# Loading the weights of a two-layer kernel through one queue, in the order keys, queries, values, output

## The chip, the cores and the metric

The kernel runs on one core of a Trainium2 chip. A core has five engines that follow their own instruction queues: TensorE (PE in the profile) multiplies matrices, VectorE (DVE) and ScalarE (ACT) work elementwise, GpSimd (POOL) builds masks and issues transfers, and SyncE (SP) does nothing here but issue transfers. Transfers between the chip's memory and the core's own memory run on 16 DMA engines, which serve the queues of SyncE, ScalarE and GpSimd. An instruction that must wait, for a transfer or for another engine, holds back everything behind it in its engine's queue.

The metric is the device time of one execution in microseconds. Before the change it is 1650.74 us, the median of three runs (1646.95 to 1651.44).

## The reference

Tokens `x` (2048 rows of 512 numbers) pass through four blocks: A, B, A, B, each with a layer normalisation in front and a residual sum behind it. Block A is attention with a small memory that is carried from segment to segment. With 32 heads of 128 and the mask "memory rows see all, tokens see what is not later":

```
mem = mem0                                   # 8 rows
for s in range(64):                          # segments of 32 tokens
    h = concat(mem, x[32 tokens of segment s])        # 40 rows of 512
    q, k, v = h @ Wq, h @ Wk, h @ Wv                  # 512 -> 32 x 128 each
    p = softmax(mask(q @ k.T * 128**-0.5))
    o = (p @ v) @ Wo                                  # 32 x 128 -> 512
    mem = o[:8]
    out[segment s] = o[8:]
```

The next segment's first eight rows are this segment's result, so the 64 segments follow each other strictly. Block B is linear attention over all 2048 tokens: `qkv = x @ wqkv`; with phi(t) = t + 1 above zero and exp(t) below it (and 1e-6 more), `kv = sum phi(k) v`, `z = sum phi(k)`, `o = phi(q) kv / (phi(q) z)`, and `o @ wo`. The same weights serve both rounds. Inputs and outputs are bf16.

## The kernel before

All weights are loaded once, at the start, and stay in the core: `Wq_sb`, `Wk_sb`, `Wv_sb` (4 MB each, partition = row of a 128-row chunk, in runs of 8 KB), `Wo_sb` (4 MB, in four loads of 8 heads, runs of 1 KB) and B's input weights `wqkv_sb` (1.5 MB). B's output weights `MB_sb` are loaded by GpSimd (`load_wo_b`, L970).

The work of block A is organised by segment (64 steps) and by tile of 128 tokens (4 segments). `prepare` (L1179) normalises a tile, transposes it with TensorE (L1075) and writes it as `hT`; `left_block` (L1138) projects the last 8 tokens of all four segments at once; `project` (L1098) is the projection of one segment: for each of four chunks of 128 rows, matmuls of the segment's rows against 512 columns of a weight, L1117 for the first and L1038 (`again`) for the following ones, which use the same loaded rows. Queries and keys are always projected together in one such instruction group, which waits for both weights. Values are projected by a group of their own. `mem_attention` (L1190) and `x_attention` (L1265) form the scores, their exponentials (ScalarE) and the weighted sums (L1050 on TensorE, L1238 and L1260 on VectorE); `out_proj` (L1339, matmuls L1353) multiplies by `Wo_sb` and waits for all four loads of it; `next_mem` (L1369) hands the eight rows on; `residual` (L1400) sends the results to their tokens with small transfers that GpSimd issues (L945). `evac` (L933) copies from the matmul accumulators, on ScalarE (L929) or VectorE (L930).

The order of the work is not found while the program runs. Every instruction is a node with a key (layer, step, name, number), and `when` (L572) looks up a time for it in two tables: `OWN` (L187) for particular steps and `PERIOD` (L19) for steps that repeat. `schedule` (L690) sorts all nodes by these times; each engine's queue is that order cut down to its own nodes. The times only sort: an instruction runs when it is at the head of its queue and what it waits for is done. The costs and latencies given to `add` (L642) are notes of a planner and do not act at run time. `finalize` (L727) turns the dependencies (`reads`, `writes`, `after`) into semaphore waits.

The start is the group with the key (0, -9, "setup"). Its first entries are the loads, in the order of the code from L955 to L971: SyncE issues the memory rows `A_mem0` and the first 128 tokens; ScalarE issues queries, keys and values, which the table sorts as values (-43583), queries (-12468), keys (-10416); SyncE issues the four output loads, the first two only after the keys have landed, the other two after the values, and then B's input weights after the output load with number 3 has landed. The table sorts the four as 1, 0, 3, 2. ScalarE's table of exponentials is loaded at L974, and all later work of ScalarE stands behind it. GpSimd loads the next two token tiles, builds constants and masks, and then stands at `load_wo_b` until B's input weights have landed.

Of the kernel before, what the change touches and what calls it, by code (L numbers as in the profile page):

```python
# [187 lines left out]
    (0, -9, 'setup'): '-23881 -2811 -12468 -10416 -43583 21376 13817 27505 24711 33310 -11418 -25383 -11486 -11353 -10564 -9986 -9510 -9028 -7908 -7700 -7486 -7329 -7314 -7002 -4822 -4403 -4292 -3436 -3097 -2480 -2001 -1544 -1040 -425 303 598 825 2114 2451 2767 3806 4244 8941 4464 5201 5238 5547 5902 10670a -9456 -7547a 39031 12088 13578 16040 16417 17105 1822 -26965',  # L188
# [6 lines left out]
    (0, 0, 'kq0'): '13808 15010 15310 17315 18082v 19746 19340a 23091',  # L195
    (0, 0, 'kq1'): '17637 18020 18543 18861 21288v 22253 21384v 23532',
    (0, 0, 'mem0'): '27658 28172 28190 29861 30676 31704 31783 32208 31967 32476',
# [12 lines left out]
    (0, 1, 'out'): '44451 44669 44741 45014 45337 45555 45773 46175 46501a 46538a',  # L210
    (0, 1, 'ql'): '32700v 32981v',
    (0, 1, 'res'): '52219 53313 54918',
    (0, 1, 'v'): '39333 40965 41700 42114 42672a 43188v',
    (0, 1, 'x'): '43625 44185 44721 45081 45683 45380 46379v 47185a 48758a 47851v 46850 47270 52096 52534 52673 53568 54508a 56814v 51794 53025 53214 53360 55042v 57491v',
    (0, 2, 'kq0'): '47407 48125 48417 49149 49383v 51153 49746a 50354',
# [5 lines left out]
    (0, 2, 'mem0'): '51902 52471 53043 53225 53347 53484 54024 54037 53671 54519',  # L221
    (0, 2, 'mem1'): '52595 52927 53142 53807 53987 54494 54953 55144 54626 55332',
    (0, 2, 'next'): '57504 57571 58118v',
    (0, 2, 'out'): '55213 55536 55596 55853 56017 56282 56453 56766 56904a 57411a',
    (0, 2, 'prep'): '7141 11551 11747 12128 13230 13879 16317v 24205a 22992v 17580a 14579a',
    (0, 2, 'ql'): '47981a 52537a',
    (0, 2, 'res'): '58281 67019 61329',
    (0, 2, 'v'): '51172 51814 51886 52975 53621v 53680a',
    (0, 2, 'x'): '54497 54743 55346 56242 56492 57902 62274a 58331v 61866a 61385a 60603 63624 63220 64197 64252 64308 64852a 69378v 63451 64157 64212 64690 65204v 66660a',
    (0, 3, 'kq0'): '58554 59210 59409 59907 60905a 60950 60138v 61209',  # L230
    (0, 3, 'kq1'): '60534 60535 60782 61428 62206a 63172 62183v 62810',
# [3 lines left out]
    (0, 3, 'out'): '65288 65592 65810 65982 66237 66316 66723 66771 67272a 67561a',  # L235
# [6 lines left out]
    (0, 4, 'mem0'): '72686 73456 74533 75009 75383 75885 77205 77353 77122 77568',  # L242
# [4 lines left out]
    (0, 4, 'res'): '80671 80824 82777 71884 72667 72775 73095 73429 74084 74354 74698 74812a 75389a 75765 80611 76852 77291 76394 79454 80754 79192 78160 84469',  # L247
    (0, 4, 'v'): '72797 75050 75264 75761 76781a 77027v',
    (0, 4, 'x'): '77272 77900 78143 78209 78737 79058 81425v 79309a 81777a 81269v 81287 81403 86062 86150 87203 87586 88466a 95437a 85646 86400 86662 86953 89440v 87687a',
# [4 lines left out]
    (0, 5, 'mem1'): '86657 86699 86929 88059 88344 88705 89233 89727 89241 90130',  # L254
# [5 lines left out]
    (0, 5, 'x'): '88077 90731 91507 91539 92846 93972 96883v 98142a 97124a 93099a 98473 95909 99150 99206 99235 99738 100206a 105270a 99879 100117 100204 100979 101797a 102570a',  # L260
    (0, 6, 'bi'): '84711 85579 85614 86087 86511 86963 86235 87472v 87874 88040 88303 88445 88757 90870 91274 114152 114458 122909 123007 125922a 126258 120139 127135 126348 123352 127014 127470 127704 127723 128959 129215 129414',
# [7 lines left out]
    (0, 6, 'mem1'): '99043 99071 99363 99702 99664 100680 101135 101181 100567 101883',  # L269
    (0, 6, 'next'): '103464 103978 104291v',  # L270
    (0, 6, 'out'): '101039 101247 101494 102002 102048 102266 102652 102763 102977a 103536a',
    (0, 6, 'prep'): '14049 14142 36561 47147 88442 88632 88768v 103149v 100817a 93747a 93965v',
    (0, 6, 'ql'): '92381a 89685a',
    (0, 6, 'res'): '104408 114484 105497',
    (0, 6, 'v'): '96416 97117 97566 98107 98450a 99368v',
    (0, 6, 'x'): '100337 101744 101969 102646 103217 103965 105837a 108154v 105947v 105369v 109602 108071 110104 110877 110951 110962 111313a 112628v 111099 111185 111472 111534 111878v 117102a',
# [4 lines left out]
    (0, 7, 'next'): '114319 114412 114889v',  # L281
# [5 lines left out]
    (0, 8, 'kq0'): '114994 115277 115928 116529 117824a 117870 118437a 118856',  # L287
# [6 lines left out]
    (0, 8, 'res'): '126874 127829 127416 118367 118620 119005 120395 120746 121165 121292 121510 121980a 122356a 122883 124485 122896 125179 122927 127002 124750 125614 127093 131320',  # L294
    (0, 8, 'v'): '119803 120314 121933 122108 122671a 123112v',
    (0, 8, 'x'): '122179 123493 123804 124525 125187 125394 125314v 128539v 127537v 125881v 133774 128307 131471 133813 134096 134138 135512v - 131116 131245 132962 134079 - 134800a',
    (0, 8, 'xl'): '89684',
    (0, 9, 'kq0'): '127940 128381 128815 129253 129992a 130193 130027v 130829',
    (0, 9, 'kq1'): '129280 129672 129761 130189 130920a 132891 130670a 132353',
    (0, 9, 'mem0'): '131377 132020 133268 133552 133420 133758 134518 134534 134256 134866',  # L300
    (0, 9, 'mem1'): '133194 133195 133862 134507 134802 135314 135480 135976 135487',
# [3 lines left out]
    (0, 10, 'bi'): '131528 132048 132423 132568 132939 133554 - 134394v 134746 134890 135163 135405',  # L305
# [12 lines left out]
    (0, 58, 'x'): '- - 760505 760834 761378 761717 765481a 762418a 766652v 761991a 767761 766509 768891 768947 769002 769058 770177a 771278a 768513 768568 768724 769776 770338v 771116a',  # L318
# [9 lines left out]
    (0, 59, 'x'): '769848 770190 770848 771439 771897 774037 772547v 772800v 772825a 773053v 775444 777039 773485 776237 776724 776779 777292a 777130a 773342 773596 777321 777377 778556a 778997a',  # L328
# [3 lines left out]
    (0, 60, 'mem1'): '779419 780681 781091 781660 781799 782529 782881 783191 782857 783541',  # L332
# [5 lines left out]
    (0, 60, 'x'): '781455 782216 782359 783392 783621 784444 784305v 784702v 784652a 784155a 786571 788051 785842 786253 786308 792585 793150a 794809a 791776 791832 791987 792266 793760v 795547v',  # L338
    (0, 61, 'kq0'): '786705 786834 787265 787696 788367v 789359 788367a 788997',
    (0, 61, 'kq1'): '788127 788558 788989 789420 790091a 790809 790572a 791249',  # L340
    (0, 61, 'mem0'): '790713 790741 791151 791539 791750 792224 792513 792949 792593 793299',
    (0, 61, 'mem1'): '791748 791887 792424 792888 793027 793303 793655 793965 793415 794315',
# [6 lines left out]
    (0, 62, 'bi'): '790202 791171 791366 791700 792549 793025 790203 794166a 795580 795796 796012 796588 797045 802425 806330 796443 817005 817236 817567 818024a 818674 818304 820023 827953 806386 806611 807178 817784 819139 820630 820951 823771',  # L349
# [7 lines left out]
    (0, 62, 'res'): '807985 809971 808991',  # L357
    (0, 62, 'v'): '800400 800831 801473 802015 803099a 802686v',
    (0, 62, 'x'): '803293 803635 804034 804871 805329 806782 806037v 805785a 805784v 806093a 807732 806926 806892 807016 807403 810316 810667a 811210v 806836 807459 811505 811563 811914v 812504a',
    (0, 63, 'kq0'): '807602 808344 809276 809587 810378v 811101 810299a 812640',  # L360
    (0, 63, 'kq1'): '808592 809885 810427 810858 812011a 812749 811529a 813111',
# [7 lines left out]
    (0, 63, 'x'): '814789 815144 815707 815910 816222 816920 817058v 817037a 817653a 817345a 817197 817942 818130 818186 818241 818297 818648a 818899 818955 819010 819066 819417v',  # L369
# [3 lines left out]
    (0, 66, 'bm'): '830386 829502 830247 830993 831337 832054 832689v 831346 831993v 831130 831586a 831838 833319a',  # L373
    (1, -6, 'bo'): '675873 795483 831613 832078 832798 833468 834212 834663 834769 834985 835444',
    (1, -4, 'start'): '660687a',
    (1, -2, 'left0'): '838552 839675 840537 841830 842501a 843585 842501v 843223',
    (1, -2, 'left1'): '838813 840106 841846 843554 844757a 845387 844275a 844906',
    (1, -2, 'lefts'): '849843 850453 850867 851285',
    (1, -2, 'leftv'): '843985 844416 844593 845278 845949a 846579 847057 846430a 847743 848013',
    (1, -2, 'prep'): '836415 836762 836957 837291 837372 838012 838482a 839279a 843047a 862887a 854362v',  # L380
    (1, 0, 'bo'): '793183 835179 838242 838490 839427 840097 849285 849741 850061 850557 852052',
    (1, 0, 'kq0'): '840968 841399 842261 843245 843794a 845749 843947v 846111',
    (1, 0, 'kq1'): '845606 846140 846295 847002 848077a 849058 847700a 848375',
    (1, 0, 'mem0'): '848295 848323 848733 849147 849285 849629 850221 850531 850277 850881',
    (1, 0, 'mem1'): '849501 849529 850006 850509 850370 850785 851137 851446 850795 851797',
    (1, 0, 'next'): '853722 853887 854257v',
    (1, 0, 'out'): '851274 851492 851710 851928 852283 852501 852856 853074 853395a 853556a',
    (1, 0, 'ql'): '845268v 846912a',
    (1, 0, 'v'): '847629 847864 848423 848737 849664a 849525v',
    (1, 0, 'x'): '850664 852162 852539 852955 853413 853752 854277a 854690v 853980a 858781a 855057 854551 859999 860055 860110 860500 861263a 863739v 859554 860199 860221 860389 861668v 863038a',  # L390
    (1, 1, 'kq0'): '854499 854930 855213 855792 856463a 857548 856463v 857186',
    (1, 1, 'kq1'): '856042 856782 857213 857645 858315v 859180 858160a 858729',
# [418 lines left out]
def _build_kernel(nc, A_x, A_mem0, A_Wq, A_Wk, A_Wv, A_Wo, A_seg_len, B_wqkv, B_wo, out):  # L811
# [112 lines left out]
    add = P.add  # L924
# [754 lines left out]
```

## Time and profile before

| | |
|---|---|
| median of three runs | 1650.74 us |
| the profiled execution's own time | 1659.31 us |
| its span, first to last instruction | 1657.6 us |
| TensorE busy | 1551.8 us, 94% of the span |
| VectorE, ScalarE, GpSimd busy | 77%, 64%, 20% |
| chain that ended last | TensorE 79%, ScalarE 8%, VectorE 7%, DMA 3% |
| mean granted TensorE clock | 0.992 |

A profile row of the timeline gives the start and the duration in microseconds, the engine (ACTq, SPq and POOLq are the issuing side of a queue, PEld is the loading of the stationary operand), the line of the kernel, the operation, the tile written and the tiles read, and in brackets the idle time of the engine before it with what ended that idle time. "pb" is the matmul accumulator; "arena" is one large tensor that holds most working tiles. Weight tiles appear by their own names, so the projections and the loads can be told apart by name. The page's first part shows where engines are busy, but the question of a start is what the first wait of each engine ended on; this is in the timeline, in the waits, and in the chain that ended last.

### The profile page before, as it was taken

To read this page: it belongs to the slowest core of one execution; us is meant where nothing else is said; L and a number is where in the kernel's file an instruction comes from. 1 tells how busy PE (TensorE), PEld (TensorE's weight loads), DVE (VectorE), ACT (ScalarE), POOL (GpSimd) and SP (SyncE) were. 2 spreads that over 40 slices of the span, in tenths; PEclk is the share of its full clock that TensorE was granted. 3 is DMA by queue.
4 is the path that set the end of the run, shared out by engine and by line. 5 is a ranking of instruction groups with operands and counts; after the bars stand their busy time and mean duration, and the time that the engine had idled before them with its cause. 6 is when DMAs were issued, how large, how long until landed. Compare 5 with 4: busy or idle time off the path is not lost.

```text
span 1657.6 us, 105934 instructions
## 1 busy us (share of the span) xinstructions
PE 1551.8 (94%) x53257; PEld 884.8 (53%) x44057; DVE 1276.4 (77%) x4017; ACT 1067.1 (64%) x3060; POOL 325.4 (20%) x660
## 2 busy tenths in 40 slices
PE   1899999999999999999799999999999999999996
PEld 0455555555555555555445555655556556555553
DVE  1677878787888787777667888787887888888766
ACT  0566666666666666666466677666767666676664
POOL 2012121222222112222102211222221221222030
PEclk9999999999999999999999999999999999999998
DMA  9300000000000000000000000000000000001013
GB/s 354 116 13 17 14 10 15 17 17 17 17 13 17 10 16 16 17 16 20 22 7 14 16 16 20 20 14 17 20 17 18 20 20 11 20 20 30 9 51 121
DMA packets 34893, 51.07 MB, mean 31 GB/s; under 512 B 13432, under 2 KB 28592, under 8 KB 32912
## 3 DMA queue, kind: packets, MB, share of 16 engines
q0 software_dynamic: 21744, 19.78, 4.1%
q1 hardware_dynamic: 11120, 11.94, 2.2%
q10 hardware_dynamic: 1584, 12.58, 1.9%
q8 instruction: 381, 6.24, 1.6%
q14 instruction: 64, 0.52, 0.1%
HBM read 29.63 MB, written 10.49 MB: 24 GB/s over the span
## 4 chain that ended last, share of the span: by engine, by line
PE 79%; ACT 8%; DVE 7%; DMA 3%; issue 2%; POOL 1%; ACTq 0%; DVEq 0%
PE pb L1117 22%; PE pb L1038 22%; PE pb L1353 16%; PE pb L1050 13%; ACT arena_sb L929 5%; DMA Wk_sb<-in_A_Wk_dram 2%; DVE arena_sb L930 2%; PE pb L1377 2%; PE pb L1211 1%; DMA dx_sb<-y_sb 1%; DVE arena_sb L1134 1%; POOL dx_sb L945 1%; PE pb L1075 1%; PE pb L1291 1%; ACT outW_sb L929 1%
## 5 line engine op out<-in xcount | busy, mean ns | idle before, releaser
L929 ACT ACTIVATE arena_sb<-pb 128x512 bf16<-128x512 f32 (+6 forms) x1068 | 505.2, 500 | 284.7 <-PE pb L1038 213.7
L945 POOL DMA_DIRECT2D dx_sb<-y_sb x504 | 252.9, 508 | 932.3 <-DVE y_sb L1388 650.3
L1050 PE MATMUL pb<-arena_sb 128*32 128x128 bf16 (+2 forms) x14320 | 404.0, 224 | 23.3 <-ACT arena_sb L929 7.3
L1117 PE MATMUL pb<-Wk_sb,arena_sb 128*32 128x512 bf16 x4096 | 413.5, 380 | 5.6 <-ACT arena_sb L929 2.9
L1038 PE MATMUL pb<-Wq_sb,arena_sb 128*32 128x512 bf16 x4096 | 413.3, 379 | 0.0
L930 DVE CAST arena_sb<-pb 128x512 bf16<-128x512 f32 (+3 forms) x647 | 335.0, 522 | 95.7 <-PE pb L1038 49.9
L1050 PEld LDWEIGHTS pb<-arena_sb 128*32 128x32 bf16 x14320 | 273.2, 96 | 200.6 <-issue 73.8
L1353 PE MATMUL pb<-Wo_sb,arena_sb 128*32 128x256 bf16 x10368 | 345.1, 273 | 6.7 <-issue 4.5
L1353 PEld LDWEIGHTS pb<-Wo_sb,arena_sb 128*32 128x32 bf16 x10368 | 264.2, 96 | 61.2 <-issue 17.8
L1134 DVE STREAM_TRANSPOSE arena_sb<-arena_sb 128x256 f32<-128x256 f32 x640 | 262.5, 431 | 25.0 <-ACT arena_sb L929 15.8
L1117 PE MATMUL pb<-Wv_sb,arena_sb 128*32 128x512 bf16 x2560 | 257.7, 378 | 0.1
L1038 PE MATMUL pb<-Wv_sb,arena_sb 128*32 128x512 bf16 x2560 | 257.6, 379 | 0.0
L1117 PEld LDWEIGHTS pb<-Wk_sb,arena_sb 128*32 128x32 bf16 x4096 | 124.7, 97 | 213.8 <-issue 169.3
L929 ACT ACTIVATE arena_sb<-arena_sb 32x256 bf16<-32x256 bf16 (+1 forms) x409 | 153.2, 378 | 22.8 <-DVE arena_sb L1298 17.2
L1117 PE MATMUL pb<-Wq_sb,arena_sb 128*32 128x512 bf16 x1024 | 107.4, 387 | 23.0 <-DMA Wk_sb<-in_A_Wk_dram 22.4
L1117 PEld LDWEIGHTS pb<-Wv_sb,arena_sb 128*32 128x32 bf16 x2560 | 76.6, 96 | 74.1 <-issue 55.7
L1228 ACT ACTIVATE arena_sb<-pb 128x192 bf16<-128x192 f32 (+1 forms) x256 | 83.8, 328 | 44.4 <-PE pb L1211 25.7
L929 ACT ACTIVATE outW_sb<-pb 128x128 fp32r<-128x128 f32 x274 | 61.9, 274 | 78.1 <-PE pb L1353 75.5
L1238 DVE TENSOR_TENSOR arena_sb<-arena_sb 128x128 bf16<-128x128 bf16 x504 | 92.7, 213 | 23.5 <-ACT arena_sb L1228 19.6
L1038 PE MATMUL pb<-Wk_sb,arena_sb 128*32 128x512 bf16 x1024 | 106.9, 386 | 0.0
L1388 DVE TENSOR_TENSOR y_sb<-pb,outW_sb 64x256 bf16<-64x256 f32 x158 | 65.8, 416 | 44.2 <-ACT outW_sb L929 39.8
L1260 DVE TENSOR_TENSOR arena_sb<-pb,arena_sb 128x128 bf16<-128x128 f32 x252 | 73.3, 291 | 34.0 <-ACT arena_sb L1249 14.7
(102 smaller groups left out, 1721.7 us busy)
## 6 DMA issues: line engine op xcount, KB each, us to landing
Wv_sb<-in_A_Wv_dram ACTq DMA_DIRECT2D x1, 4096.0 KB, 14.0
Wq_sb<-in_A_Wq_dram ACTq DMA_DIRECT2D x1, 4096.0 KB, 23.3
Wk_sb<-in_A_Wk_dram ACTq DMA_DIRECT2D x1, 4096.0 KB, 32.6
Wo_sb<-in_A_Wo_dram SPq DMA_DIRECT2D x4, 1024.0 KB, 10.4
xs_scratch<-x_sb POOLq DMA_DIRECT2D x32, 128.0 KB, 2.0
pq_scratch<-arena_sb POOLq DMA_DIRECT2D x32, 128.0 KB, 2.0
dx_sb<-y_sb POOLq DMA_DIRECT2D x252, 12.0 KB, 1.9
dx_sb<-y_sb POOLq DMA_DIRECT2D x252, 4.0 KB, 1.9
```

Source lines behind the costliest of these rows:

```text
L929: return e.activation(o() if callable(o) else o, i() if callable(i) else i, ACTF.Copy)
L930: return e.tensor_copy(o() if callable(o) else o, i() if callable(i) else i)
L945: add(eng, lambda e: e.dma_start(o, i), 0.55 if eng == "pool" else 0.4, reads=reads, writes=writes, dsem="%s%d" % (kind, k), lat=lat + (0. ...
L1038: return pe.add_instruction(mybir.InstMatmult(name=nc.get_next_instruction_name(), engine=mybir.EngineType.PE, ins=[pe.lower_ap(x), pe.low ...
L1050: r = pe.matmul(o[q], w[:, q], x, start=start, stop=stop, skip_group_check=True, tile_position=(0, 32 * j))
L1117: r = pe.matmul(o, blk[:, c, :], w, start=(c == 0), stop=(c == 3), tile_position=(0, 32 * j))
L1134: add("dve", lambda v: v.transpose(dst, src(img[:, k, :].bitcast(F32))), 0.445, reads=[("img", k)], writes=[dkey])
L1228: add("act", lambda a: a.activation(PQ[:, r2, b, 0:nq], tl.f32()[:, 0:nq], ACTF.Exp, scale=SCALE), c_act(nq), tiles=[tl], writes=[("PQ", r ...
L1238: add("dve", lambda v, a=a, p_=p_, w_=w_: v.tensor_tensor(wide(Pm[:, k, a, :]), p_.unsqueeze(2).to_broadcast([128, 4, 4, 8]), w_, ALU.mult ...
L1260: add("dve", lambda v: v.tensor_tensor(oTb[:, s % NO, 16 * b:16 * b + 16, 0:8], pv.f32()[:, 0:128].rearrange("p (n q) -> p n q", q=8), Rm[ ...
L1353: r = pe.matmul(tl.f32()[32 * j:32 * j + 32, 0:256], oT[:, 4 * hh + n, :], Wo_sb[:, 8 * n + hh, 256 * d:256 * d + 256], start=(hh == 0 and ...
L1388: add("dve", lambda v: v.tensor_tensor(y_sb[0:64, k, :], tl.f32()[0:64, 0:256], outW[64:128, w, :].bitcast(F32), ALU.add), c_dve(256), rea ...
```

## The change

SyncE's queue takes all weight loads, in the order keys, queries, values, output weights 0 to 3, B's input weights. None waits for the landing of another; only their order in the queue is fixed. The memory rows and the first tokens move to ScalarE's queue, ahead of its table load. In the `OWN` table the ten load entries become the ten smallest times. The other changed entries of the table, 154 of them, move by 1.

```
     (0, -9, 'setup'): '-23881 -2811 -12468 -10416 -43583 21376 13817 27505 24711 33310 -11418 ...      # before
     (0, -9, 'setup'): '-1000000 -999999 -999998 -999997 -999996 -999995 -999994 -999993 -999992 -999991 -11418 ...   # after
```

```diff
     P.at(0, -9, "setup")
-    add("sp", lambda s: s.dma_start(mem0_sb[0:M, :], A_mem0[0]), 0.1, writes=[MEM0], dsem="dmem", lat=2.0)
-    add("sp", lambda s: s.dma_start(x_sb[:, 0, :], x_view[0]), 0.4, writes=[("x", 0)], dsem="dx0", lat=8.5)
+    add("act", lambda a: a.dma_start(mem0_sb[0:M, :], A_mem0[0]), 0.45, writes=[MEM0], dsem="dmem", lat=2.5)
+    add("act", lambda a: a.dma_start(x_sb[:, 0, :], x_view[0]), 0.45, writes=[("x", 0)], dsem="dx0", lat=6.0)
     late = []
-    for i, (W, v, nm, t) in enumerate(((Wq_sb, qk_view[0], "Wq", 13.2), (Wk_sb, qk_view[1], "Wk", 23.7),
-                                       (Wv_sb, qk_view[2], "Wv", 34.8))):
-        late.append(add("act", lambda a, W=W, v=v: a.dma_start(W[:, :, :], v), 0.5, writes=[nm], dsem="d" + nm, lat=t))
+
+    def load(o, i, nm, lands):
+        late.append(add("sp", lambda e: e.dma_start(o, i), 0.45, writes=[nm], dsem="d%d" % len(late),
+                        lat=lands - 1.25 - 0.45 * len(late)))
+        late[-1].order.update(late[-2:-1])
+
+    for W, v, nm, t in ((Wk_sb, qk_view[1], "Wk", 14.2), (Wq_sb, qk_view[0], "Wq", 24.0), (Wv_sb, qk_view[2], "Wv", 33.8)):
+        load(W[:, :, :], v, nm, t)
     wo_view = A_Wo.rearrange("h e d -> e h d")
     for i in range(4):
         hs = slice(8 * i, 8 * i + 8)
-        add("sp", lambda s, hs=hs: s.dma_start(Wo_sb[:, hs, :], wo_view[:, hs, :]), 0.9, writes=[("Wo", i)],
-                 dsem="dWo%d" % i, after=[late[1 + i // 2]], lat=(12.5, 14.5, 7.3, 9.8)[i])
-    add("sp", lambda s: s.dma_start(wqkv_sb[:, :, :], B_wqkv.rearrange("(c p) f -> p c f", p=128)), 0.5,
-        writes=["wqkv"], dsem="dwqkv", after=[P.nodes[-1]], lat=5.0)
-    late.append(P.nodes[-1])
+        load(Wo_sb[:, hs, :], wo_view[:, hs, :], ("Wo", i), 36.9 + 3.1 * i)
+    load(wqkv_sb[:, :, :], B_wqkv.rearrange("(c p) f -> p c f", p=128), "wqkv", 50.0)
...
     P.before["act"] = add("act", lambda a: a.preload_act_table_set("natural_log_exp_and_others"), 1.3)
+    P.before["act"].order.update(P.nodes[0:2])
```

`late[-1]`, on which GpSimd's `load_wo_b` waits, is B's input weights as before.

## The prediction

> **What bounds the kernel now.** I read the DMA issues first (KB each, us from issue to landing), because the change touches nothing but loads at the start.
>
> ```profile
> Wv_sb<-in_A_Wv_dram ACTq DMA_DIRECT2D x1, 4096.0 KB, 14.0
> Wq_sb<-in_A_Wq_dram ACTq DMA_DIRECT2D x1, 4096.0 KB, 23.3
> Wk_sb<-in_A_Wk_dram ACTq DMA_DIRECT2D x1, 4096.0 KB, 32.6
> ```
>
> With the issues at 0.81, 1.28 and 1.87 us (timeline), the big weights land at 14.8, 24.6 and 34.5: values, queries, keys. The steps of 9.8 and 9.9 us show that they are served one after the other, 4.19 MB at about 425 GB/s. Next the chain that ended last, in order of time (start, duration):
>
> ```profile
> 1.87 32.59 DMA Wk_sb<-in_A_Wk_dram
> 34.50 0.62 PE pb L1117 x3
> ```
>
> and who waited for whom in the first 120 us (total us, times, longest):
>
> ```profile
> PE pb L1117 <- DMA Wk_sb<-in_A_Wk_dram: 22.4, 1, 22.4
> ...
> SPq L964 <- DMA Wk_sb<-in_A_Wk_dram: 32.9, 1, 32.9
> SPq L966 <- DMA Wo_sb<-in_A_Wo_dram: 7.3, 1, 7.3
> ...
> POOL arena_sb L971 <- DMA arena_sb<-in_B_wqkv_dram: 40.3, 1, 40.3
> ```
>
> TensorE idles 22.4 us until the keys land, and this wait is on the chain: its first 34.5 us are loading. After that TensorE is the bound (94% busy, 79% of the chain). The timeline of the start (start, duration, instruction, idle before it and its releaser):
>
> ```profile
> 9.28 0.69 DVE L1061 BATCH_NORM_STATS2 st_sb<-x_sb 128x6 f32<-128x512 bf16 x1 [7.82 <-DMA x_sb<-in_A_x_dram]
> ...
> 12.83 0.39 ACT L929 ACTIVATE arena_sb<-pb 128x96 bf16<-128x96 bf16 x2 [0.16 <-DVE arena_sb L930]
> ...
> 34.50 0.62 PE L1117 MATMUL pb<-Wq_sb,arena_sb 128*32 128x512 bf16 x4 [22.41 <-DMA Wk_sb<-in_A_Wk_dram]
> ...
> 44.80 0.10 PEld L1117 LDWEIGHTS pb<-Wv_sb,arena_sb 128*32 128x32 bf16 x4 [0.33 <-issue]
> ...
> 55.63 1.93 PE L1353 MATMUL pb<-Wo_sb,arena_sb 128*32 128x256 bf16 x64
> 55.74 0.77 POOL L971 DMA_DIRECT2D arena_sb<-in_B_wo_dram  x1 [40.30 <-DMA arena_sb<-in_B_wqkv_dram]
> ...
> 58.31 0.35 PE L1050 MATMUL pb<-arena_sb 128*32 128x128 bf16 x12 [0.76 <-ACT arena_sb L929]
> ...
> 75.45 1.03 POOL L945 DMA_DIRECT2D dx_sb<-y_sb  x2 [18.94 <-DVE y_sb L1388]
> ```
>
> It shows when each weight is wanted: queries and keys together at 34.5, values 10.3 us later, output weights 21.1 us later. The values land first and lie unused for 30 us. The tokens are ready at 13.2.
>
> **The change part by part.** The three big loads keep their size and stay in one queue; the order becomes keys, queries, values. The first matmul then needs the second load instead of the third and can start at 24.6 instead of 34.5: **gain 9.9 us**. Behind it the order of every engine is that of before: the other entries of the table move by at most 1, and where this makes or breaks a tie, the two entries belong to different engines. So I shift every row after 34.5 by 9.9 and ask which load then comes too late.
>
> Values: wanted at 44.8 - 9.9 = 34.9; as third load they land at about 34.5. **Cost 0**, with 0.4 us to spare; each us of delay beyond that costs one.
>
> Output weights: wanted at 55.6 - 9.9 = 45.7. They follow the values in the same queue, without the gap after 34.5 in which little moved. Their rate is in the stretches (last number GB/s, before it the DMA share):
>
> ```profile
> 33.00:34.00 1.00, 0.00 (x0) 0.00 (x0) 0.00 (x0) 0.00 (x0) 0.00 (x0) 1.00 0.66 270
> ...
> 41.00:42.00 1.00, 1.00 (x26) 0.22 (x12) 0.00 (x0) 0.00 (x0) 0.00 (x0) 1.00 1.02 335
> ...
> 46.00:47.00 1.00, 1.00 (x28) 0.24 (x12) 1.00 (x5) 0.25 (x1) 0.00 (x0) 1.00 1.10 347
> ```
>
> The third big load's bytes end near 33.7 (270 of 425 GB/s in that stretch). From 37 to 48 the output weights run at 345 GB/s on average, so their 4.19 MB take 12.2 us and end at 45.9. From last bytes to landing took 0.8 us for the keys and 1.5 for the last of the four output loads (bytes end about 49.0, landing 50.5): they land at 46.7 to 47.4, take 47.0. TensorE stalls from 45.7 to 47.0. What waits behind: after its 64 matmuls TensorE waited another 0.76 us for ScalarE (row at 58.31), whose work runs on during the stall, so 0.75 us of it is cover. **Cost 0.5 us** (0.2 to 1.0; without that cover 1.3).
>
> ScalarE's queue loses three issues (0.44, 0.53 and 0.50 us) and takes over two (0.38 and 0.36 us on SyncE). The token load is issued at about 1.3 instead of 1.24. It landed at 9.2 amid the values' traffic; the chain from it to ready tokens took 4.0 us, so it may land as late as 20.6 before 24.6 is touched. The 8 KB of memory tokens lie under the same cover. **Cost 0**.
>
> SyncE issues eight loads back to back. The four of the output weights took 5.93 us to issue when their queue was filling, and SyncE may stall longer now; behind them it has nothing until the loads of the last stage, near 1590. **Cost 0**. B's input weights follow: 1.57 MB at 359 to 419 GB/s (stretches 50 to 53) is 3.9 us, landing near 50.6. GpSimd stands in its queue waiting for that at L971, and its next transfer is the one of 75.45, now 65.6: **cost 0**, with 14 us of cover.
>
> TensorE's clock is a two-sided unknown. The first 4.6 us of matmuls ran slow: 0.62 to 0.64 us each until 39.08, then 0.38. [...] I take the row, 0. The granted clock stands at 1.00 in these stretches and cannot show it.
>
> [...]
>
> The sum: -9.9 + 0 + 0.5 + 0 = **-9.4 us**. The profiled span of 1657.6 (the execution's own time is 1659.31) becomes 1648.2. The plain runs' median, 1650.74, lies 8.6 below that execution; the start is on the chain in any execution and I take the same 9.4 off: **1641.3 us**, 0.57% faster. A difference under 0.3% (5.0 us) is about what the measurement cannot tell from none.
>
> **The rivals.** First, the output weights come late. From issue to last landing they took 34.5 to 50.5, 16.0 us; if that and not the rate holds after the values, they land at 34.4 + 16.0 = 50.4, 4.0 later than the 46.4 that the cover allows: gain 5.9, **1644.8**. For it: SyncE's issues stalled up to 3.2 us. Against: with a full queue the first three us of low rate (56, 193, 313 GB/s) have no reason.
>
> Second, the change does not do what it says: on SyncE's queue the three loads share the engines instead of following each other, and keys and queries land when all do, near 34.5: **1650.7**, no change. Against: the equal steps of landing on the other queue, and the first output load on SyncE's queue landing at 40.2, the last at 50.5.
>
> Third, slower: the token load on ScalarE's queue is starved by the queue that SyncE fills. It costs nothing until it lands at 20.6, makes the kernel slower than before from 30.5 on (34.5 - 4.0), and measurably from 35.5. If it waits for all bytes queued by SyncE up to the output weights (47.0), the first matmul starts at 51.0, 16.5 later than now: **1667.2**. For it: before, it took 8.0 us where a small transfer takes 2. Against: that was under the same full traffic, and GpSimd's two token loads landed in 6.0 and 7.0 us under it, so each queue got its turn.
>
> **How the numbers follow.** Forecast 0.76; late output weights 0.12; loads sharing 0.07; starved tokens 0.05. Faster: 0.95 of the first, 0.65 of the second (it lies 0.9 us beyond the bound), sum 0.80. Slower: the starved tokens, 0.05. The same: the rest, 0.15. The likeliest case gains 7.8 to 10.3 by its bounds, 1640.4 to 1642.9; the medians of before and after can each be off by some 2 us (its three runs span 4.5). The range takes in the first rival: **1637.5 to 1647.0**.
>
> **What would show it.** First matmul on queries and keys at 24 to 25 us, behind a wait of about 12.5 on the queries; values' first use near 35 with no wait on the load; a wait of 1.0 to 1.7 us at L1353 near 46, its releaser the output weights; L971 near 51; from the second segment on every row 9 to 10 us earlier, and the span shorter by as much. I am wrong if the first matmul starts after 26, if a wait for values or output weights exceeds 2 us, if normalisation of the first tokens starts after 17, or if the shift at 100 us is not found again at the end.

## The result and the profile after

The changed kernel takes 1644.7 us (median of 12 runs, 1638.41 to 1647.87) against 1650.57 us for the kernel before in the same runs (12, 1646.95 to 1654.44). The ratio is 0.9959, with an interval of 0.9948 to 0.9970: 0.41% faster, 5.0 to 8.6 us. The forecast was 1641.3, that is 9.4 us: the direction was right and the size too large, since the medians fell by 5.9 us and the ratio is worth 6.8.

The spans of the two profiled executions, 1657.6 and 1638.8 us, differ by 18.8. Single executions of one kernel lie up to 9.5 us apart (the runs above), and the profiled execution of before, 1659.31, lies above all 12 of its runs, so this difference is no measure of the change. What can be read from two traces is where the same instruction stands in each. The changed kernel has three more lines ahead of the engine code, so L1117 is now L1120, L1353 is L1356 and L971 is L973. First the loads again (KB each, us from issue to landing):

```profile
Wk_sb<-in_A_Wk_dram SPq DMA_DIRECT2D x1, 4096.0 KB, 13.6
Wq_sb<-in_A_Wq_dram SPq DMA_DIRECT2D x1, 4096.0 KB, 23.1
Wv_sb<-in_A_Wv_dram SPq DMA_DIRECT2D x1, 4096.0 KB, 33.8
```

With the issues at 0.81, 1.29 and 1.84 they land at 14.4, 24.4 and 35.6. The order is the intended one; but the third load needs 1.1 us more than the third load of before, which landed at 34.5. The timeline of the changed kernel shows where TensorE stood:

```profile
24.43 0.62 PE L1120 MATMUL pb<-Wq_sb,arena_sb 128*32 128x512 bf16 x4 [11.88 <-DMA Wq_sb<-in_A_Wq_dram]
...
29.43 0.64 PE L1120 MATMUL pb<-Wq_sb,arena_sb 128*32 128x512 bf16 x4
...
35.18 0.38 PE L1041 MATMUL pb<-Wk_sb,arena_sb 128*32 128x512 bf16 x4
...
35.77 0.40 PE L1120 MATMUL pb<-Wv_sb,arena_sb 128*32 128x512 bf16 x4 [0.21 <-issue]
...
47.72 1.93 PE L1356 MATMUL pb<-Wo_sb,arena_sb 128*32 128x256 bf16 x64 [1.57 <-DVE arena_sb L930]
...
50.03 0.25 PE L1380 MATMUL pb<-selm_sb,outW_sb 128*32 128x16 f32 x8 [0.21 <-ACT outW_sb L929]
...
51.94 0.24 PE L1053 MATMUL pb<-arena_sb 128*32 128x128 bf16 x4 [1.19 <-issue]
...
68.19 1.03 POOL L945 DMA_DIRECT2D dx_sb<-y_sb  x2 [15.65 <-DVE y_sb L1391]
```

The start has moved as forecast, but the gain shrinks from mark to mark. The releaser named at 47.72 is a copy by VectorE that ended at 47.58. This projection does not need it: in the kernel before the same copy ran at 56.88, after the projection had started. The VectorE work that it does need (L1263, L1260 before) ended at 46.06. The last of the four output loads, issued at 35.77, took 11.9 us to land (the smallest of the three figures below) and came in at 47.63, so it was the load.

```profile
DMA to landing us min/median/max: 11.9/22.4/36.3
```

For the last marks of the table, the rows of before behind the output projection:

```profile
58.52 0.26 PE L1377 MATMUL pb<-selm_sb,outW_sb 128*32 128x16 f32 x8
...
59.26 0.40 PE L1117 MATMUL pb<-Wk_sb,arena_sb 128*32 128x512 bf16 x4
```

| mark | before | after | earlier by | forecast |
|---|---|---|---|---|
| first projection, queries and keys | 34.50 | 24.43 | 10.07 | 9.9 |
| last of them ahead of the values | 44.80 | 35.18 | 9.62 | 9.9 |
| first matmul on the values | 45.02 | 35.77 | 9.25 | 9.9 |
| first output projection | 55.63 | 47.72 | 7.91 | 8.6 |
| the 12 matmuls behind it | 58.31 | 49.47 | 8.84 | 9.4 |
| memory rows handed on | 58.52 | 50.03 | 8.49 | 9.4 |
| second segment's projection | 59.26 | 52.00 | 7.26 | 9.4 |
| GpSimd's first result transfer | 75.45 | 68.19 | 7.26 | 9.4 |

From the second segment on the shift stays: GpSimd's next transfers stand 7.26 us earlier, up to that of 99.4. 7.3 us is inside the interval of the ratio. In a second profiled execution of the same kernel the transfer of 75.45 stands at 68.10, 7.35 earlier. Further on single executions drift apart by more than the experiments below differ: at the transfer of 162.6 the two stand 6.9 and 7.6 us earlier, at that of 786 they stand 11.5 and 8.8. So a shift is read at 75 us, and does not say what is left of it at the end.

### The profile page after: what moved, and what is told of

Same layout as the page of the kernel before. It is cut to its first block, busy times and chain, and to the rows that moved or that the text cites. A ratio compares the mean times of both kernels' runs of the same rounds, so it can differ in the third digit from the quotient of the medians.

```text
span 1638.8 us, 105934 instructions
## 1 busy us (share of the span) xinstructions
PE 1545.9 (94%) x53257; PEld 881.7 (54%) x44057; DVE 1276.5 (78%) x4017; ACT 1068.0 (65%) x3060; POOL 326.3 (20%) x660
## 4 chain that ended last, share of the span: by engine, by line
PE 80%; ACT 8%; DVE 7%; DMA 2%; issue 2%; POOL 0%; DVEq 0%; SPq 0%
PE pb L1120 22%; PE pb L1041 22%; PE pb L1356 17%; PE pb L1053 13%; ACT arena_sb L929 5%; DVE arena_sb L930 2%; PE pb L1380 2%; PE pb L1214 1%; DMA Wq_sb<-in_A_Wq_dram 1%; DVE arena_sb L1137 1%; DMA dx_sb<-y_sb 1%; PE pb L1078 1%; PE pb L1294 1%; ACT outW_sb L929 1%; DVE arena_sb L1241 1%
## 5 line engine op out<-in xcount | busy, mean ns | idle before, releaser
L1120 PE MATMUL pb<-Wk_sb,arena_sb 128*32 128x512 bf16 x4096 | 412.7, 380 | 4.5 <-ACT arena_sb L929 2.7
L1356 PE MATMUL pb<-Wo_sb,arena_sb 128*32 128x256 bf16 x10368 | 343.1, 273 | 6.8 <-issue 2.8
L1356 PEld LDWEIGHTS pb<-Wo_sb,arena_sb 128*32 128x32 bf16 x10368 | 263.7, 96 | 60.5 <-issue 15.2
L1120 PE MATMUL pb<-Wv_sb,arena_sb 128*32 128x512 bf16 x2560 | 257.4, 378 | 0.2 <-issue 0.2
L1120 PEld LDWEIGHTS pb<-Wk_sb,arena_sb 128*32 128x32 bf16 x4096 | 124.0, 97 | 212.0 <-issue 169.3
L1120 PE MATMUL pb<-Wq_sb,arena_sb 128*32 128x512 bf16 x1024 | 106.9, 388 | 11.9 <-DMA Wq_sb<-in_A_Wq_dram 11.9
L1120 PEld LDWEIGHTS pb<-Wv_sb,arena_sb 128*32 128x32 bf16 x2560 | 76.6, 96 | 73.9 <-issue 55.4
L1263 DVE TENSOR_TENSOR arena_sb<-pb,arena_sb 128x128 bf16<-128x128 f32 x252 | 73.3, 291 | 34.2 <-ACT arena_sb L1252 15.1
```

What stands on the lines that cost most here:

```text
L1120: r = pe.matmul(o, blk[:, c, :], w, start=(c == 0), stop=(c == 3), tile_position=(0, 32 * j))
L1263: add("dve", lambda v: v.tensor_tensor(oTb[:, s % NO, 16 * b:16 * b + 16, 0:8], pv.f32()[:, 0:128].rearrange("p (n q) -> p n q", q=8), Rm[ ...
L1356: r = pe.matmul(tl.f32()[32 * j:32 * j + 32, 0:256], oT[:, 4 * hh + n, :], Wo_sb[:, 8 * n + hh, 256 * d:256 * d + 256], start=(hh == 0 and ...
```

## The experiments

Each was compared with the kernel before on its own chip. The medians of before lie between 1651 and 1659 on these chips; only ratios and places in the trace are compared. "Shift" means how much earlier than before (75.45 us) GpSimd's first result transfer starts.

**The queue without the order.** The changed kernel with the old order of the three loads:

```diff
-    for W, v, nm, t in ((Wk_sb, qk_view[1], "Wk", 14.2), (Wq_sb, qk_view[0], "Wq", 24.0), (Wv_sb, qk_view[2], "Wv", 33.8)):
+    for W, v, nm, t in ((Wv_sb, qk_view[2], "Wv", 14.2), (Wq_sb, qk_view[0], "Wq", 24.0), (Wk_sb, qk_view[1], "Wk", 33.8)):
```

> The changed kernel with the old order of the three big loads: values, queries, keys, all on SyncE's queue, no waits. My theory: the first matmul waits for the third load, which in the changed kernel landed 1.1 us later than the third load of the kernel before, because the output weights stand behind it in the same queue; so the first matmul starts near 35.6, everything is about 1 us later than before (1651 to 1652, not to be told from before). Rival (the queue without waits brings the gain): 5 us or more faster than before. If the third load lands at 34.5, what follows it in the queue does not hold it back and the 1.1 us have another cause.

Measured: ratio 0.9999 (0.9988 to 1.0010), shift 0.1 us. The timeline of this kernel:

```profile
34.49 0.62 PE L1120 MATMUL pb<-Wq_sb,arena_sb 128*32 128x512 bf16 x4 [22.15 <-DMA Wk_sb<-in_A_Wk_dram]
...
55.55 1.93 PE L1356 MATMUL pb<-Wo_sb,arena_sb 128*32 128x256 bf16 x64 [0.52 <-DVE arena_sb L1263]
```

Queue and missing waits alone bring nothing. And the third load lands at 34.5 although the output weights stand behind it, so my first reason for the late values (what follows in the queue holds them back) falls. Here TensorE was idle during the third load, there it was at work.

**The order without the queue.** The kernel before, with keys and values exchanged on ScalarE's queue; the output weights still wait for landings:

```diff
-    (0, -9, 'setup'): '-23881 -2811 -12468 -10416 -43583 21376 ...
+    (0, -9, 'setup'): '-23881 -2811 -12468 -43583 -10416 21376 ...
...
-                 dsem="dWo%d" % i, after=[late[1 + i // 2]], lat=(12.5, 14.5, 7.3, 9.8)[i])
+                 dsem="dWo%d" % i, after=[late[2 - i // 2]], lat=(12.5, 14.5, 7.3, 9.8)[i])
```

> The kernel before with one thing changed: the three big loads stay on ScalarE's queue but come in the order keys, queries, values, and the output weights still wait for landings (two for the last of the three, two for the first). My theory (the order moves the start, the missing gap moves the output weights): first matmul on queries and keys at 24.4 to 24.6 us, values landing near 34.5 with no wait of TensorE on them, the last output load landing near 50.5 as before, so that the first matmul on them starts near 50.5 and not near 46; from there on everything 5 to 6 us earlier than before, time 1644 to 1646. Rival (the queue and the missing waits bring the gain, the order does not): first matmul near 34.5, no difference in time. Second rival (the order is all of it): 9 us earlier than before, 1641.

Measured: ratio 0.9997 (0.9987 to 1.0007), shift 2.2 us, which lies at the edge of that interval. All three expectations missed the size. The start moved fully, and was lost again:

```profile
24.43 0.62 PE L1117 MATMUL pb<-Wq_sb,arena_sb 128*32 128x512 bf16 x4 [12.55 <-DMA Wq_sb<-in_A_Wq_dram]
...
51.48 3.60 PE L1353 MATMUL pb<-Wo_sb,arena_sb 128*32 128x256 bf16 x64 [5.31 <-issue]
...
55.46 0.31 PE L1377 MATMUL pb<-selm_sb,outW_sb 128*32 128x16 f32 x8
```

The values landed at 35.6 again, so the output weights were issued at 35.62 and the last came at about 51.3: 4.2 us gained at that point. After 5.3 idle us the granted clock is 0.50, from 49.56 to 56.39, and the same 64 matmuls took 3.60 instead of 1.93 us. In part this fell into the wait that stood behind them before (0.76 us at 58.31): the memory rows are handed on 3.1 us earlier, the second segment starts 2.2 earlier. Order alone brings 2.2 us, queue alone 0.1, both together 7.3: the order pays only if the output weights follow at once.

This kernel also shows why the values are late, since nothing stands behind them here. Its stretches (us, the five engines, clock, DMA share, GB/s), and the DMA queues from 25 to 35 us:

```profile
33.00:34.00 1.00, 1.00 (x24) 0.25 (x12) 0.88 (x2) 0.57 (x1) 0.00 (x0) 1.00 0.59 229
34.00:35.00 1.00, 1.00 (x20) 0.10 (x4) 0.83 (x3) 0.03 (x1) 0.00 (x0) 1.00 0.07 16
```

```profile
q10 hardware_dynamic: 453, 3.59, 86.4%
q8 instruction: 1, 0.02, 0.7%
```

In the last us a share of 0.07 is one of 16 DMA engines, which alone still moves 16 KB, two runs of the values. And one instruction packet of 16 KB was loaded in this time. It started at 33.02 and took 1.08 us; a run of the weights, 8 KB, takes 0.32. It ended at 34.10, and the two runs that were still left started at 34.08 and 34.88, when those of all other engines had started by 33.43. So one engine was busy with instructions for 1.1 us, and the load had landed only when this engine was done. In the changed kernel a packet of the same size started at 32.72 and took 1.09 us, and the values landed at 35.6 there too. In the traces of the kernel before and of the queue-only kernel no instruction packet lies between 25 and 35 us, and the third load landed at 34.5 in both.

**Longer runs for the output weights.** Each partition reads 32 consecutive rows, in runs of 8 KB:

```diff
-    wo_view = A_Wo.rearrange("h e d -> e h d")
+    wo_view = A_Wo.rearrange("h (a b) d -> (h a) b d", a=4)
```

> The changed kernel, with the output weights read in runs of 8 KB instead of 1 KB: each partition reads 32 consecutive rows, so the rows of the output weights stand in the wrong places and the output is not the reference's; bytes, instructions and waits are the same. My theory (the 345 GB/s of the output weights come from their short runs, and they set the start of the first output projection): their 4.19 MB pass at about 425 GB/s, the last lands at 45 to 46, TensorE's wait of 1.6 us ahead of the first output projection falls under 0.3, and the shift there is about 9.5 us instead of 7.9. The values land nearer to 34.5 too if short runs behind them held them back. Rival (the rate is limited by something other than the runs): landing stays near 47.7 and the wait stays. Time 1 to 2 us under the changed kernel.

Measured: ratio 0.9948 (0.9932 to 0.9963), shift 9.1 us.

```profile
35.64 0.40 PE L1120 MATMUL pb<-Wv_sb,arena_sb 128*32 128x512 bf16 x4 [1.01 <-DVE arena_sb L1137]
...
45.96 1.93 PE L1356 MATMUL pb<-Wo_sb,arena_sb 128*32 128x256 bf16 x64 [0.21 <-DVE arena_sb L1263]
```

The output of this kernel is not the reference's; bytes and waits are the same. The values were as late as ever, a second sign that the short runs are not what held them. The wait ahead of the output projection fell from 1.6 to 0.2 us: runs of 1 KB at some 345 GB/s set its start in the changed kernel, where runs of 8 KB moved 416 GB/s here (mean from 34 to 46 us). The layout is not a free choice in this kernel, whose output projection reads a head's 128 numbers from the partitions.

**B's input weights later.** They are issued after the last matmul of the first output projection (and sorted there):

```diff
+    gate = [n for n in P.nodes if n.engs == ("pe",) and n.key == (0, 0, "out", 7)]
+    late[-1].sync.add(gate[0])
     P.schedule()
```

> The changed kernel, with B's input weights issued only after the last matmul of the first output projection. Theory of instruction fetch: the 1.2 us in which TensorE waits at 50.7 for nothing that the profile shows come from a 16 KB instruction packet that starts 1 us late because these 1.5 MB fill the DMA engines; without them the packet starts earlier, the idle time falls under 0.3 us, and from the second segment on everything is 8.3 to 8.6 us earlier than before (7.3 in the changed kernel). Rival (the idle time belongs to the place in the program and to what came before, not to the traffic): 1.2 us stay, and the shift stays 7.3. The output weights land as in the changed kernel, near 47.7. Time 1 us under the changed kernel or the same, too little to be told by time alone.

Measured: ratio 0.9959 (0.9944 to 0.9974), shift 8.2 us. The wait in question:

```profile
51.05 0.24 PE L1053 MATMUL pb<-arena_sb 128*32 128x128 bf16 x4 [0.43 <-issue]
```

The 1.19 us became 0.43. The instruction packet ahead of it starts at 48.7 here and at 49.3 in the changed kernel, where B's weights kept the DMA engines full until about 49.5 (share 1.06 from 48 to 49 us, 0.06 here); the output projection itself stood only 0.13 us apart in the two. So the traffic of B's weights costs about 0.8 of the 1.2 us. That it does so by delaying the packet fits the 0.7 us by which the packet starts earlier, but is not shown apart from that. 0.4 remain, more than the 0.3 I expected at most; what they wait for is not shown. In time no difference from the changed kernel shows.

**TensorE kept busy ahead of the start.** 130 matmuls on a constant tile while the weights load:

```diff
+    P.at(0, -9, "warm")
+    tl = P.tile()
+    for i in range(WARM):
+        add("pe", lambda t, tl=tl: t.matmul(tl.f32()[:, 0:128], id_sb[:, :], id_sb[:, :], start=True, stop=True), 0.06,
+            reads=["id"], tiles=[tl])
```

> The changed kernel with 130 extra matmuls of 128x128 on a constant tile, issued by TensorE between the first tokens' transposes and the first projection, while the weights load; their result is not used. Theory (one instruction packet of 16 KB occupies one DMA engine for 1.1 us, and a load has landed only when its slowest engine is done; the packets follow TensorE's progress through its instructions): the extra instructions draw a packet before the queries have landed, so the first projection starts near 25.5 instead of 24.4, and a second packet near 33 holds the values back again. The slow matmuls of the first 5.4 us (0.62 to 0.64 us) are gone, 0.38 from the start, so queries and keys are done at about 33 and the wait for values grows to 2 to 3 us. The first output projection still starts when its weights have landed, 47.6 to 48.7: the time is that of the changed kernel, within 1 us. Rival (the slow clock costs time at the end): about 2.5 us faster than the changed kernel. Rival to the packets (something else made the values late): first projection at 24.4.

Measured: ratio 0.9945 (0.9927 to 0.9963), shift 7.4 us.

```profile
12.38 9.89 PE L1034 MATMUL pb<-id_sb 128*128 128x128 bf16 x130
25.66 0.62 PE L1128 MATMUL pb<-Wq_sb,arena_sb 128*32 128x512 bf16 x4 [3.38 <-issue]
...
47.80 1.93 PE L1364 MATMUL pb<-Wo_sb,arena_sb 128*32 128x256 bf16 x64 [0.87 <-DVE arena_sb L1310]
```

With the extra instructions an instruction packet starts at 21.08, where the changed kernel has none ahead of 32.72, and the queries landed 1.2 us later (first projection 25.66 for 24.43), as the theory of the packets said. The purpose failed: the filler ended at 22.3, and after 3.4 idle us the first projections were slow again (the granted clock is 0.50 from 24.42 to 31.24), so what a fast clock would bring was not tested here. 1.2 us lost at the start cost nothing at 47.80, since the output weights come when they come. The shift is that of the changed kernel (7.3 to 7.4); that the ratio looks better lies within the intervals, and rests on four runs.

**The loads in pieces.** Keys and queries alternate in pieces of 128 rows, values and output weights come in pieces too, each matmul group waits for its own piece, and B's input weights come later as above:

```diff
+    for c in range(4):
+        load(Wk_sb[:, c, :], qk_view[1][:, c, :], ("Wk", c), 14.2)
+        load(Wq_sb[:, c, :], qk_view[0][:, c, :], ("Wq", c), 24.0)
+    for c in range(4):
+        load(Wv_sb[:, c, :], qk_view[2][:, c, :], ("Wv", c), 33.8)
...
+    for i in range(8):
+        load(Wo_sb[:, i::8, :], wo_view[:, i::8, :], ("Wo", i), 36.9 + 1.5 * i)
...
-                add("pe", mm, 0.218, reads=[("Wo", i) for i in range(4)] + keys[hh // 4], tiles=[tl])
+                add("pe", mm, 0.218, reads=[("Wo", hh)] + keys[hh // 4], tiles=[tl])
```

> The changed kernel with the loads in pieces and with waits to match: keys and queries alternate in pieces of 128 rows (1 MB), values likewise, the output weights in eight pieces by the head that one group of the output projection multiplies, each group waiting for its own piece; B's input weights are issued after the first output projection. Theory (the landing of the output weights sets the start of everything after it): the first projection begins near 13 us on the first pieces and is paced by the loads; the groups of the output projection run as their pieces land and the last ends 0.3 to 0.6 us after the last landing at about 47.7, at 48.2 and not at 49.65; from the second segment on everything is 9 to 10 us earlier than before, 2 us less than the changed kernel: ratio to before about 0.994. Rival (small pieces cost more in the DMA engines than they bring): the last landing comes later than 48.7 and nothing is gained over the changed kernel.

Beside it ran the changed kernel once more.

> The changed kernel itself, as the measure for the kernel beside it on the same chip. Both theories: 0.4 to 0.5% faster than before, as the trace of it shows 7.3 us of 1650; the first segments' marks as in its first profile (first projection 24.4, values 35.8, output projection 47.7).

Measured: the changed kernel 0.9967 (0.9955 to 0.9980), shift 7.35; the pieces 0.9937 (0.9920 to 0.9953), shift 8.6 us, a little short of 9.

```profile
43.53 1.69 PE L1361 MATMUL pb<-Wo_sb,arena_sb 128*32 128x256 bf16 x48
46.22 0.40 PE L1361 MATMUL pb<-Wo_sb,arena_sb 128*32 128x256 bf16 x8 [1.00 <-DMA Wo_sb<-in_A_Wo_dram]
47.56 0.40 PE L1361 MATMUL pb<-Wo_sb,arena_sb 128*32 128x256 bf16 x8 [0.94 <-DMA Wo_sb<-in_A_Wo_dram]
...
49.12 0.68 PE L1125 MATMUL pb<-Wk_sb,arena_sb 128*32 128x512 bf16 x4
...
52.34 0.40 PE L1125 MATMUL pb<-Wk_sb,arena_sb 128*32 128x512 bf16 x4
```

Six of eight groups of the output projection are done before the last pieces land, and the memory rows are handed on at 48.35, 10.2 us earlier than before. The landings also separate the packet from TensorE's work as such, the rival that the earlier runs leave open: the first piece of the values landed 2.48 us behind the last of the queries and the others 2.49, 3.83 and 2.53 us behind one another, while TensorE was busy all the time, and the one instruction packet of this time, 29.97 to 31.07, falls into the long step. Then the second segment's matmuls run at half speed for 3 us: the row at 49.12 shows 0.68 us, and they start 0.43 us apart instead of 0.22. Eight such groups (49.12 to 52.34 is 3.2 us, where 59.26 to 60.99 of before is 1.7) cost 1.5 us. The stretches around it, in the columns used above:

```profile
45.30:48.72 3.42, 1.34 (x58) 0.89 (x62) 0.68 (x2) 1.42 (x5) 0.00 (x0) 1.00 0.12 43
48.72:52.13 3.41, 3.41 (x61) 1.08 (x34) 0.54 (x2) 0.98 (x3) 0.00 (x0) 0.50 0.86 276
```

The granted clock is 0.50 from 48.72 to 52.13. In all ten traces its changes lie whole multiples of 3.41 us apart. In the last such stretch before this change TensorE was busy 1.34 of 3.42 us, 39%. Taking every stretch of the ten traces up to the end of the work, those at full clock that were followed by half were busy 47% or less, and those followed by full clock 45% or more. The longest wait does not sort them: in the trace of before the stretch from 49.52 to 52.94 held one wait of 1.87 us, was 45% busy (1.55 us) and was followed by full clock, while no wait here exceeded 1.00 us. So in these traces the slow clock goes with all idle time of one stretch together, and where the stretches lie differs from execution to execution (full clock first came 5.7 us after the first projection in one execution of the changed kernel and 4.6 in the other).

**Pieces, with the two waits filled.** Seven matmuls on data that have landed, 4 in front of the last but one group and 3 in front of the last:

```diff
+    P.at(0, 0, "fill")
+    tl = P.tile()
+    for i in range(FILL):
+        add("pe", lambda t, tl=tl: t.matmul(tl.f32()[:, :], id_sb[:, :], Wk_sb[:, 0, 0:512], start=True, stop=True), 0.22,
+            reads=["id", ("Wk", 0)], tiles=[tl])
```

> The kernel with loads in pieces, and seven matmuls of 128x512 on constant data, unused, put in front of the last two groups of the first output projection, where TensorE waited 1.00 and 0.94 us for the last two pieces of the output weights. Theory (these two waits, with the ones before them, brought the slow clock, which held the next 8 groups of matmuls from 48.6 to 52.1 at 0.43 us instead of 0.22 and cost 1.5 us): with the waits filled, the projections of the second segment run at 0.22 us each from the start, and the shift against before stays 10.0 to 10.2 us to the end of the first tile instead of 8.6; ratio to before near 0.993. Rival (the slow stretch comes with the free-running phase or from elsewhere): matmuls of 0.6 us remain after 48 and the shift stays near 8.6.

Measured: ratio 0.9945 (0.9928 to 0.9961), shift 10.0 us.

```profile
45.13 1.04 PE L1649 MATMUL pb<-Wk_sb,id_sb 128*128 128x512 bf16 x4
...
47.57 0.40 PE L1363 MATMUL pb<-Wo_sb,arena_sb 128*32 128x256 bf16 x8 [0.18 <-DMA Wo_sb<-in_A_Wo_dram]
...
49.09 0.40 PE L1127 MATMUL pb<-Wk_sb,arena_sb 128*32 128x512 bf16 x4
```

The same projection starts at the same time and runs at full speed, and the shift is 1.4 us larger. That the unused work kept the clock up is not shown, because this execution would have kept it by the figures above in any case: its stretches run from 42.64 to 46.05 and from 46.05 to 49.46, TensorE was busy 3.04 and 2.95 us in them, and without the 0.92 and 0.94 us of the unused matmuls at least 59% would be left. In the stretch of the pieces the same matmuls would have raised 39% to near 90% (an estimate from 1.34 + 1.7 of 3.42 us), so by this estimate they would have helped there; the rival, that the slow clock came by how the stretches happened to lie, stands beside it. By place in the trace this is the best of the versions at 75 us, 10.0 us ahead of before against 7.3 for the changed kernel; at the transfer of 162.6 it stands 8.4 us ahead and the pieces 8.8. By time both versions in pieces beat the kernel before, and which of the two is faster the ratios cannot say. Against the changed kernel, the pieces lie lower on the same chip (1639.46 against 1645.0 us in the medians), with intervals that just miss each other at 0.9953 and 0.9955.

## Why the prediction was right in direction and too large

**The gain at the start, 9.9 us**: right, 10.07 in the trace. The wait was on the path, and it went.

**Values, "cost 0" with 0.4 us to spare**: wrong by 0.4 us at this place. They landed 1.1 us later than the row of before said. That row was taken while TensorE stood still. In the changed kernel and in the order-only kernel, where TensorE worked during the third load, an instruction packet held one DMA engine for 1.09 and 1.08 us and the load landed at 35.6; in the kernel before and in the queue-only kernel no packet lies there, and it landed at 34.5. The step that failed is the shift of every row by 9.9: I asked which load comes too late and left the loading of instructions out of the loads.

**The clock, taken as 0**: 0.45 lost at this place, by chance. The slow matmuls lasted from 24.43 to about 29.9, 5.4 us instead of 4.6. The bounds of the likeliest case, 7.8 to 10.3, hold 0.6 gained and 1.1 lost for the clock, which no run shows. What the runs showed in their place: in the seven traces that start with the whole loads and no filler, full clock came 3.7 to 6.0 us after the first projection, 4.8 in the trace of before. In the slow time the matmul groups start 0.43 us apart instead of 0.22, so half of a difference is lost or gained: 0.5 gained to 0.6 lost (an estimate from these figures). Later in the program it was not the length of a single wait that went with a slow stretch: in the pieces kernel none there exceeded 1.00 us and yet a slow stretch followed. The measurement points to the busy share of a stretch of 3.41 us (39% there).

**The rate of the big loads, about 425 GB/s from the rows**: right for the first two; the queries landed as second load at 24.4, where 24.6 was taken, 10.0 us behind the keys (419 GB/s).

**Output weights, "cost 0.5 us"**: they landed at 47.6, 0.2 us behind the range of 46.7 to 47.4 and 0.6 behind the 47.0 that was taken. The cover is mis-sized too. All of the 0.75 us that TensorE had to spare was used up at the matmuls at 49.47; and the copy of the output projection's result on ScalarE, hidden behind ScalarE's other work before, was no longer hidden and cost 0.35 more (8.84 earlier there, 8.49 at the handing on). From the 9.51 by which TensorE's last matmuls of the earlier work led (the five at 45.51 in place of 55.02), 1.02 was lost at this place, where I had 0.5.

**What no step had**: 1.2 us at 50.7, where TensorE waited for nothing that the profile shows. I had costed the back-to-back issue of B's weights at 0 because nobody needs them early. Moving them away took 0.8 of it back.

In TensorE's rows the losses add up: 0.45 for the clock, 0.37 for the values, 0.26 back from a shorter unnamed wait at 45.5, 1.02 for the output weights and what hangs on them, 1.23 at the unnamed wait of 50.7, together 2.81, and 10.07 - 2.81 = 7.26. But what was lost ahead of 47.6 did not cost time at the end, since the output weights set the start of what follows. In the second execution of the changed kernel full clock came 4.6 us after the first projection instead of 5.7; TensorE then waited 0.61 us for the values instead of 0.21, began the output projection at 47.64 for 47.72, and the second segment at 51.92 for 52.00. In the warm kernel 1.2 us more were lost at the start, with the same end. So of the forecast 9.4 these are missing: 0.56 where the output weights landed later than taken (8.84 at the matmuls behind them), 0.35 for ScalarE's copy, and 1.23 for the unnamed wait, which no term of the sum had. 9.4 - 2.14 = 7.26.

The remaining step from 7.3 in the trace to 5.9 in the medians is inside the interval and was not pursued.

**The rivals.** That the measured 1644.7 lies on the first rival's 1644.8 is chance. The output weights that take 16.0 us came true in the order-only kernel (issued at 35.62, there at 51.3), and not in the changed kernel, where they follow without a gap. Loads that share the engines, and starved tokens, did not occur: the loads landed one after the other, and the first tokens' normalisation began at 9.75 instead of 9.28. (GpSimd's two token loads took 6.5 and 6.0 us in the trace of before, not 6.0 and 7.0; the argument stays.) That the range up to 1647.0 took in the result is owed to the room left for the first rival: the bounds of the likeliest case, 1640.4 to 1642.9, did not. The sign "found again at the end" cannot be read from two single executions that scatter by more than the change; it rests on the ratio.

## What to carry to other kernels

At a start that waits for weights, order the loads by first use and let the next one follow without a gap: here the order alone brought 2.2 us, the queue alone 0.1, both 7.3. Expect that a load can come later than in a trace in which the engines stood still meanwhile: here the third load landed at 35.6 instead of 34.5, with an instruction packet on one of its DMA engines for 1.1 us. Put loads that nobody needs yet behind the first critical stretch (0.8 of 1.2 us of waiting went with that here). When a stage hangs on the landing of a load, ask of each loss on which side of the landing it lies: here 1.2 us more ahead of it left no trace (warm), 1.2 us behind it stayed. Let each part wait for its own piece, and look at the matmul durations and the clock after the waits: a gain at the landing can be lost again to a slow clock (1.5 us of it in the pieces).

## What was not expected of the hardware

- A single instruction packet of 16 KB took 1.09 us of one DMA engine in the changed kernel and 1.08 in the order-only kernel, and in both the third load of 4 MB landed 1.1 us later than in the two traces without a packet there (35.6 for 34.5). With 130 more instructions of TensorE ahead of the start a packet came at 21.08 and the first projection, which waits for the queries, at 25.66 instead of 24.43.
- Two waits of 1.00 and 0.94 us close together were followed by 3 us of matmuls at half speed. The stretch of 3.41 us before it was 39% busy; in all ten traces the stretches that kept the full clock were busy 45% or more, and one of 47% was followed by half.
- At the start the granted clock reads 1.00 while matmuls take 0.62 to 0.64 us for 0.38 to 0.40: the clock records begin only at 39.28 us in the trace of before and at 30.13 in that of after, where the durations fall to 0.38, and up to there only the durations show that the matmuls ran slow. Later the column does show it: 0.50 from 48.72 to 52.13 in the pieces and from 49.56 to 56.39 in the order-only kernel.
